# Linear attention with a gated one-token FFN: kv times wo in full matmuls, an earlier normalisation, and another order of the first loads

## The chip, the cores and the metric

The kernel runs on one core of one Trainium2 chip. The metric is the time on the device in microseconds (us), median of three runs. A profile of one execution stands beside it, with a trace of every instruction. TensorE is the matrix engine (PE in the profile, PEld its weight loads), VectorE is DVE, ScalarE is ACT, GpSimd is POOL, and SyncE (SP) issues most of the transfers. Each engine works through its own queue in order and waits for others by semaphores.

## The reference

The input x has 2048 tokens of 1024 numbers, in bf16. Path A is linear attention with 32 heads of 32 numbers; path B feeds the one token with the highest router score through a gated FFN and adds the result to that token alone; a sigmoid gate per token mixes the two. Cut to what matters:

```python
qkv = x @ wqkv                                  # 2048 x 3072, split in q, k, v of 32 heads x 32
phi = lambda t: where(t > 0, t + 1, exp(t)) + 1e-6
pq, pk = phi(q), phi(k)
kv  = einsum("bhsd,bhse->bhde", pk, v)          # 32 x 32 for each head
z   = einsum("bhsd->bhd", pk)
num = einsum("bhqd,bhde->bhqe", pq, kv)
den = einsum("bhqd,bhd->bhq", pq, z) + 1e-6
a   = (num / den) @ wo                          # heads side by side, then 1024 x 1024
# B: idx = argmax(x @ w_r); y = (silu(x[idx] @ w_gate) * (x[idx] @ w_up)) @ w_down
#    b = x with sigmoid(r[idx]) * y added to row idx
g   = sigmoid((x * gate_w).sum(-1))
out = g * a + (1 - g) * b
```

The kernel never forms num: it divides pq by den, multiplies kv by wo once (M, 1024 x 1024), and the output is pq times M.

## The kernel before

P is 128, D 1024, NG and KC are 8 (groups of 128 columns, four heads each), NT is 16 (tiles of 128 tokens). The start: loads, the transposes of the first two x tiles on TensorE, and the first K products, which run along with the K rows of the weights as they land.

```python
    load_x(0, 1)
    load_k(0)
    load_x(1, 1)
    for c in range(1, KC):
        load_k(c)
    for t in (2, 3):
        sp.dma_start_transpose(out=xT[:, :, t * P : (t + 1) * P], in_=x2d[t * P : (t + 1) * P, :])
    for c in (0, 4):
        sp.dma_start(out=wkv[:, c : c + 4, D : 2 * D], in_=wqkv_v[:, c : c + 4, 2 * D : 3 * D])
...
    warm_sb = const.tile([P, 512], BF)
    dve.memset(warm_sb[:], 0.0)
...
    def phi_exp(ps):
        u = tmp.tile([P, 512], F32, tag="phi_u")
        act.activation(u[:], ps, ACTF.Relu, scale=-1.0, bias=LN1EPS)
        e = tmp.tile([P, 512], F32, tag="phi_e")
        act.activation(e[:], u[:], ACTF.Exp, scale=-1.0, bias=LN1EPS)
        return e

    def phi_dve(ps, e0, out_ap):
        dve.scalar_tensor_tensor(out_ap, ps, EPS, e0[:], op0=ALU.max, op1=ALU.add)
...
    def unit_Q(g, j, pinned=False):      # phi of 128 columns of q for 512 tokens, transposed
        ps = ps_work.tile([P, 512], F32, tag="w")          # ps_work: four PSUM banks
...
    def warm(n):
        for _ in range(n):
            pe.matmul(warm_ps[:], lhsT=warm_sb[:, 0:P], rhs=warm_sb[:], start=True, stop=True)

    warm(N_WARM)
...
    def first_mm(t, c0, c1):
        for c in range(c0, c1):
            for nb in range(2):
                kv_mm(first[t][nb], t, nb, c, c + 1)
...
    unit_T(0)
    first_mm(0, 0, 1)
    unit_T(1)
    warm(1)
    for c in range(1, KC):
        first_mm(0, c, c + 1)
        if c < KC - 1:
            first_mm(1, c - 1, c)
    es = [phi_exp(first[0][nb][:]) for nb in range(2)]
...
    for t in (2, 3):
        kv_open(t)
        for nb in range(2):
            ps = ps_t.tile([P, 512], F32, tag="t")
            kv_mm(ps, t, nb, 0, KC)
            kv_evac(ps, t, nb)
```

After that come V of the first four tiles, the router, K, V and kv sums of the other twelve with Q units and the FFN among them (not touched by the change). Then the part between the last kv sum and the output:

```python
    for i in range(3):
        n = 3 if i < 2 else 2
        acc3 = kvacc[i][:, 0 : 129 * n].rearrange("p (g e) -> p g e", e=129)
        dve.tensor_copy(kvbd[:, 3 * i : 3 * i + n, :], acc3[:, :, 0:128])
...
    wo = pb.tile([P, 2, 4, D], BF)
    wo_v = A_wo.rearrange("(hf r c e) n -> hf r e c n", hf=2, r=4, c=4)
    for hf in range(2):
        for r in range(4):
            nc.sync.dma_start(out=wo[32 * r : 32 * r + 32, hf, :, :], in_=wo_v[hf, r])
    kvT = pb.tile([P, 2, 4, 32], BF)
...
    def den_group(pair):                 # denominators of 1024 tokens, 16 matmuls, then
...                                      # dn on ScalarE, and on VectorE
        dve.reciprocal(rd[:], dn[:])
        for hh in range(4):
            eng = nc.sync if hh % 2 == 0 else nc.gpsimd
            eng.dma_start(out=rdp[pair][32 * hh : 32 * hh + 16, :], in_=rd[hh : P : 8, :])
        return rdp[pair]
...
    def norm_step(n):
        for _ in range(n):
            if not norm_units:
                return
            rd, g, j = norm_units.popleft()
            rb = tmpb.tile([P, 512], F32, tag="rb", bufs=4)
            dve.stream_shuffle(rb[:], rd[:], [8 * (j % 2) + g] * 32)
            sl = pq_all[:, g, 512 * j : 512 * j + 512]
            nc.gpsimd.tensor_tensor(sl, sl, rb[:], op=ALU.mult)

    def unit_M(hf, nh):
        pm = [ps_den.tile([P, 512], F32, tag="d", name=f"pm{r}") for r in range(3)]
        pm.append(ps_ffn.tile([P, 512], F32, tag="f", name="pm3"))
        strict[0] = True
        for c in range(4):
            for r in range(4):
                pe.matmul(pm[r][32 * c : 32 * c + 32, :], lhsT=kvT[32 * r : 32 * r + 32, hf, c, :],
                          rhs=wo[32 * r : 32 * r + 32, hf, c, 512 * nh : 512 * nh + 512],
                          start=True, stop=True, tile_position=(32 * r, 32 * c))
        strict[0] = False
        for r in range(4):
            eng = dve.tensor_copy if r % 2 else act.copy
            eng(m_sb[:, 4 * hf + r, 512 * nh : 512 * nh + 512], pm[r][:])

    rdA = den_group(0)
    unit_Q(*q_units.popleft())
    pt = ps_den.tile([P, NG, P], BF, tag="d")
    for g in range(NG):
        pe.transpose(pt[:, g, :], kvbd[:, g, :], ident[:])
    for c in range(4):
        for r in range(4):
            eng = dve.tensor_copy if r % 2 else act.copy
            eng(kvT[32 * r : 32 * r + 32, :, c, :], pt[32 * c : 32 * c + 32, r:NG:4, 32 * c : 32 * c + 32])
    normalise(rdA, 0)
    normalise(rdA, 1)
    g_m = 0
    nq_done = 0
    while q_units:
        unit_Q(*q_units.popleft(), pinned=True)
        nq_done += 1
        if g_m < 4 and nq_done > 5 and nq_done % 2 == 0:
            unit_M(g_m // 2, g_m % 2)
            g_m += 1
        if nq_done % 3:
            norm_step(1)
...
    for t in range(NT):                  # output: 16 matmuls of 512 columns for each tile
...
            for g in range(NG):
                pe.matmul(ps[:, 0:cw], lhsT=pq_all[:, g, t * P : (t + 1) * P], rhs=m_sb[:, g, c0 : c0 + cw], ...)
            dve.scalar_tensor_tensor(ot[:, c0 : c0 + cw], ps[:, 0:cw], gate[:, t : t + 1], xg[:, c0 : c0 + cw], ...)
...
        if t == 0:
            rdB = den_group(1)
            normalise(rdB, 2)
            normalise(rdB, 3)
        norm_step(NORM_PER_T[t])
```

A normalisation step is a shuffle on VectorE, which spreads a row of reciprocals over the partitions of its head, and a multiplication on GpSimd in place; the output matmul of a tile needs it for all eight groups. ps_work has four banks, ps_ffn one; ps_t (three banks) serves the start and ps_den (three) the end. Where `strict[0]` is set, TensorE keeps program order; elsewhere a scheduler places the instructions when the program is built.

## Time and profile before

| what | value |
|---|---|
| time, median of 3 | 263.29 us (262.69 to 263.72) |
| span of the profiled run | 261.1 us |
| TensorE | 250.6 us busy, 96% |
| VectorE | 151.4 us, 58% |
| ScalarE | 125.4 us, 48% |
| GpSimd | 46.4 us, 18% |
| matmul for K and V, 128x512 | 465 in the records |
| matmul for the output, 128x512 | 259 in the records |
| multiplication on GpSimd, 128x512 | 32, 1163 ns each |
| shuffle on VectorE, 128x512 | 32, 733 ns each |
| reciprocal on VectorE, 128x512 | 2, 3.35 us each |

A few per cent of the matmul records are missing from the trace. The end of a matmul is modelled: one of 512 columns is shown with 379 ns, but the next one starts 0.2157 us after it at full clock, so counts are multiplied by the distance of the starts. In lines of a group the columns are: line, engine, operation, output and input, shapes and count, then busy time with the mean of one, then the idle time of the engine ahead of it and what ended it. In a timeline the first column is the start and the second the length, both in us. Nearly all instructions go through one recording helper and so carry its line, L75; they are told apart by the names of their tiles.

### The profile page before, as it was taken

The page shows a single profiled execution, that of the slowest core. Times are in us where ns is not written, and L with a number is a line of the kernel's source. Part 1 is how long each engine was busy: PE and PEld are TensorE (multiplying, and loading weights), DVE is VectorE, ACT ScalarE, POOL GpSimd, SP SyncE. Part 2 cuts the span into 40 slices and gives each one's busy share as a digit, 9 for nine tenths or more (in the row PEclk, how much of TensorE's full clock was granted, in tenths as well). Part 3 has the DMA queues.
Part 4 walks back from the last instruction along what each step waited for, and adds up shares of the span by engine and source line. Part 5 has one row for each costly group of instructions (what it writes and reads, how often), then busy time and mean ns, then how long its engine had stood idle before and what let it go on. Part 6 is the DMA issues. An engine that isn't in the chain of part 4 may idle for free.

```text
span 261.1 us, 3892 instructions
## 1 busy us (share of the span) xinstructions
PE 250.6 (96%) x1444; PEld 115.8 (44%) x1471; DVE 151.4 (58%) x254; ACT 125.4 (48%) x202; POOL 46.4 (18%) x94
## 2 busy tenths in 40 slices
PE   7999999999999999999999999999995999999994
PEld 4444454444444444444444444444441344444443
DVE  1055033323173326699999942587599699974443
ACT  2195324646445354445553735579883442242310
POOL 5000001010000000000000000110059469990000
PEclk9999999999999999999999999999999799999999
DMA  6999980029999989997970000990001174545222
GB/s 221 268 343 233 227 321 1 0 13 350 348 348 343 326 263 335 348 392 250 465 251 0 3 0 0 248 209 9 3 1 40 45 252 128 161 151 173 80 80 80
DMA packets 47369, 47.71 MB, mean 183 GB/s; under 512 B 18476, under 2 KB 35252, under 8 KB 47288
## 3 DMA queue, kind: packets, MB, share of 16 engines
q1 hardware_dynamic: 47064, 47.34, 60.0%
q8 instruction: 11, 0.18, 0.3%
q0 software_dynamic: 256, 0.14, 0.2%
q14 instruction: 6, 0.05, 0.1%
q10 hardware_dynamic: 32, 0.00, 0.0%
HBM read 39.34 MB, written 8.40 MB: 183 GB/s over the span
## 4 chain that ended last, share of the span: by engine, by line
PE 74%; DVE 14%; issue 3%; POOL 3%; DMA 3%; ACT 2%; DVEq 0%; POOLq 0%; SPq 0%
PE ps L75 65%; DVE yacc L75 10%; POOL pq_all L556 3%; DMA wt<-in_B_w_down_dram 3%; PE first L75 3%; PE kvacc L75 2%; ACT u L75 1%; DVE pk L75 1%; PE warm_ps L75 1%; DVE rb L75 1%; ACT e L75 1%; PE dps L75 1%; DVE pq_all L75 1%; PE rps L75 1%; PE pst L75 0%
## 5 line engine op out<-in xcount | busy, mean ns | idle before, releaser
L75 PE MATMUL ps<-wkv,xT 128*128 128x512 bf16 x465 | 107.1, 379 | 1.2 <-DVE pk L75 0.4
L75 PEld LDWEIGHTS <-xT 128*128 128x128 bf16 x512 | 48.8, 98 | 59.9 <-issue 5.0
L75 PE MATMUL ps<-m_sb,pq_all 128*128 128x512 bf16 (+1 forms) x259 | 57.3, 379 | 3.4 <-POOL pq_all L556 2.2
L75 PE MATMUL ps<-xT,wq 128*128 128x512 bf16 x250 | 57.5, 379 | 0.9 <-issue 0.5
L75 ACT ACTIVATE u<-ps 128x512 f32<-128x512 f32 x60 | 35.8, 596 | 38.5 <-PE ps L75 37.2
L75 ACT ACTIVATE e<-u 128x512 f32<-128x512 f32 x64 | 40.3, 630 | 2.3 <-DVE pq_all L75 0.4
L75 PEld LDWEIGHTS <-pq_all 128*128 128x128 bf16 x264 | 25.9, 99 | 34.5 <-POOL pq_all L556 4.7
L556 POOL TENSOR_TENSOR pq_all<-pq_all,rb 128x512 bf16<-128x512 bf16 x32 | 36.1, 1163 | 20.3 <-PE ps L75 17.8
L75 PEld LDWEIGHTS <-wq 128*128 128x128 bf16 x256 | 24.5, 98 | 30.3 <-issue 2.0
L75 ACT CAST vt<-ps 128x512 bf16<-128x512 f32 x32 | 18.8, 587 | 36.0 <-PE ps L75 34.8
L75 DVE SCALAR_TENSOR_TENSOR yacc<-wt,hcol,yacc 128x1024 f32<-128x1024 bf16 x27 | 34.5, 1279 | 0.5
L75 DVE SCALAR_TENSOR_TENSOR pq_all<-ps,e 128x512 bf16<-128x512 f32 x32 | 21.9, 685 | 18.9 <-ACT e L75 18.6
L75 DVE SCALAR_TENSOR_TENSOR ot<-ps,gate,xg 128x512 bf16<-128x512 f32 (+1 forms) x33 | 23.7, 725 | 15.7 <-PE ps L75 15.7
L75 DVE SCALAR_TENSOR_TENSOR pk<-ps,e 128x512 bf16<-128x512 f32 x28 | 19.1, 685 | 21.9 <-ACT e L75 21.9
L75 ACT ACTIVATE xg<-xt,omg 128x1024 f32<-128x1024 bf16 x16 | 18.1, 1146 | 25.8 <-DVE ot L75 25.8
L75 DVE STREAM_SHUFFLE rb<-rdp 128x512 f32<-128x512 f32 x32 | 22.2, 733 | 0.0
L205 POOL MEMSET vt<- 128x8 bf16 x16 | 1.9, 137 | 108.4 <-PE kvacc L75 108.4
L75 PEld LDWEIGHTS <-pk 128*128 128x128 bf16 x128 | 8.5, 98 | 3.3 <-issue 0.4
L75 PE MATMUL kvacc<-vt,pk 128*128 128x129 bf16 x128 | 9.7, 221 | 0.0
L75 PE MATMUL first<-wkv,xT 128*128 128x512 bf16 x31 | 7.8, 400 | 0.1
L75 DVE SCALAR_TENSOR_TENSOR pk<-first,e 128x512 bf16<-128x512 f32 x4 | 2.8, 692 | 8.6 <-ACT e L75 8.6
L75 DVE CAST r_bf<-rps 128x512 bf16<-128x512 f32 x1 | 0.7, 690 | 12.0 <-PE rps L75 12.0
(97 smaller groups left out, 87.5 us busy)
## 6 DMA issues: line engine op xcount, KB each, us to landing
wt<-in_B_w_down_dram SPq DMA_DIRECT2D x14, 512.0 KB, 6.4
wt<-in_B_w_gate_dram SPq DMA_DIRECT2D x8, 512.0 KB, 8.1
wt<-in_B_w_up_dram SPq DMA_DIRECT2D x8, 512.0 KB, 8.7
xt<-xp SPq DMA_DIRECT2D x16, 256.0 KB, 3.1
out_dram<-ot SPq DMA_DIRECT2D x15, 256.0 KB, 2.0
wt<-in_B_w_gate_dram SPq DMA_DIRECT2D x8, 384.0 KB, 6.8
wt<-in_B_w_up_dram SPq DMA_DIRECT2D x8, 384.0 KB, 5.4
wkv<-in_A_wqkv_dram SPq DMA_DIRECT2D x8, 256.0 KB, 4.7
```

Source lines behind the costliest of these rows:

```text
L75: inst = fn(*a, **k)
L205: nc.gpsimd.memset(vt_t[t][:, :, 128:129], 1.0)
L556: nc.gpsimd.tensor_tensor(sl, sl, rb[:], op=ALU.mult)
```

## The change

It has four parts. First, kv times wo: before, the 32x32 blocks of kv are cut out of the transposed matrix by 16 small copies and multiplied with permuted rows of wo by sixteen tiles of the array at once; now kv is multiplied by a block-diagonal mask on the way out of PSUM, transposed whole, and each group of 128 rows is multiplied with its own 128 rows of wo by two full matmuls, whose results all leave through ScalarE. wo comes in its natural order by one transfer. Second, the normalisation: one step after every Q unit, not after two of three, and another table of steps for the output tiles; Q units are no longer pinned to program order. Third, the start: the clock of TensorE is warmed on constants that exist when the program starts, instead of on a tile that VectorE has to clear; two K rows of the weights are loaded and used ahead of the second x tile, and narrow warming matmuls stand before them. Fourth, the K sums of the fourth token tile go to the work banks instead of the three banks of the transposes. The aim is fewer waits of TensorE at the start and ahead of the output.

```diff
--- before.py
+++ after.py
@@ -28,11 +28,11 @@
 NG = D // P
 EPS = 1e-6
 LN1EPS = math.log1p(EPS)
-N_WARM = 5
+N_WARM = 6
 Q_PER_T = {4: 2, 5: 1, 6: 1, 7: 2, 8: 1, 9: 1, 10: 2, 11: 1, 12: 1, 13: 2, 14: 1, 15: 0}
 FFN_PER_T = {6: (0, 4), 7: (4, 4), 8: (4, 4), 9: (4, 4), 10: (4, 2), 11: (2, 2), 12: (1, 2), 13: (1, 2), 14: (1, 2), 15: (1, 0)}
 FFN_DEPTH = 9
-NORM_PER_T = [2, 2, 2, 2, 2, 2, 2, 2, 2, 2, 2, 1, 0, 0, 0, 0]
+NORM_PER_T = [2, 0, 0, 3, 3, 3, 3, 3, 3, 3, 3, 3, 3, 3, 3, 3]
 
 
 @with_exitstack
@@ -125,8 +125,9 @@
 
     load_x(0, 1)
     load_k(0)
+    load_k(1)
     load_x(1, 1)
-    for c in range(1, KC):
+    for c in range(2, KC):
         load_k(c)
     for t in (2, 3):
         sp.dma_start_transpose(out=xT[:, :, t * P : (t + 1) * P], in_=x2d[t * P : (t + 1) * P, :])
@@ -136,13 +137,14 @@
         sp.dma_start_transpose(out=xT[:, :, 512 * g4 : 512 * g4 + 512], in_=x2d[512 * g4 : 512 * g4 + 512, :])
     sp.dma_start(out=wq[:], in_=wqkv_v[:, :, 0:D])
 
-    warm_sb = const.tile([P, 512], BF)
-    dve.memset(warm_sb[:], 0.0)
-
     ident = const.tile([P, P], BF)
     make_identity(nc, ident[:])
     nc.scalar.dma_start(out=wrg_rows[0:8, :], in_=B_w_r.rearrange("(c p) -> c p", p=P))
     nc.scalar.dma_start(out=wrg_rows[8:16, :], in_=gate_w.rearrange("(c p) -> c p", p=P))
+    mask_bd = const.tile([P, P], F32)
+    nc.gpsimd.memset(mask_bd[:], 0.0)
+    for i in range(4):
+        nc.gpsimd.memset(mask_bd[32 * i : 32 * i + 32, 32 * i : 32 * i + 32], 1.0)
     nc.gpsimd.memset(mzc[:], 0.0)
     for hh in range(4):
         for g0 in range(4):
@@ -227,20 +229,21 @@
                              start=False, stop=False, skip_group_check=True)
         del pk_t[t], vt_t[t]
 
-    def unit_Q(g, j, pinned=False):
+    def unit_Q(g, j):
         ps = ps_work.tile([P, 512], F32, tag="w")
-        strict[0] = pinned
         for c in range(KC):
             pe.matmul(ps[:], lhsT=wq[:, c, g * P : (g + 1) * P], rhs=xT[:, c, 512 * j : 512 * j + 512],
                              start=(c == 0), stop=(c == KC - 1))
-        strict[0] = False
         phi_evac(ps[:], pq_all[:, g, 512 * j : 512 * j + 512])
 
     warm_ps = ps_ffn.tile([P, 512], F32, tag="f")
 
-    def warm(n):
+    warm_w = nc.const_aps.tensor(1.0, (P, P), BF)
+    warm_x = nc.const_aps.tensor(1.0, (P, 512), BF)
+
+    def warm(n, w=512):
         for _ in range(n):
-            pe.matmul(warm_ps[:], lhsT=warm_sb[:, 0:P], rhs=warm_sb[:], start=True, stop=True)
+            pe.matmul(warm_ps[:, 0:w], lhsT=warm_w, rhs=warm_x[:, 0:w], start=True, stop=True)
 
     warm(N_WARM)
     kv_open(0)
@@ -253,13 +256,14 @@
                 kv_mm(first[t][nb], t, nb, c, c + 1)
 
     unit_T(0)
-    first_mm(0, 0, 1)
+    warm(3, 128)
+    first_mm(0, 0, 2)
     unit_T(1)
-    warm(1)
-    for c in range(1, KC):
+    for c in range(2, KC):
         first_mm(0, c, c + 1)
         if c < KC - 1:
-            first_mm(1, c - 1, c)
+            first_mm(1, c - 2, c - 1)
+    first_mm(1, 5, 6)
     es = [phi_exp(first[0][nb][:]) for nb in range(2)]
     first_mm(1, 6, 8)
     for nb in range(2):
@@ -269,7 +273,8 @@
     for t in (2, 3):
         kv_open(t)
         for nb in range(2):
-            ps = ps_t.tile([P, 512], F32, tag="t")
+            pool, tag = (ps_t, "t") if t == 2 else (ps_work, "w")
+            ps = pool.tile([P, 512], F32, tag=tag)
             kv_mm(ps, t, nb, 0, KC)
             kv_evac(ps, t, nb)
     ps_t_cm.__exit__(None, None, None)
@@ -503,17 +508,15 @@
     for i in range(3):
         n = 3 if i < 2 else 2
         acc3 = kvacc[i][:, 0 : 129 * n].rearrange("p (g e) -> p g e", e=129)
-        dve.tensor_copy(kvbd[:, 3 * i : 3 * i + n, :], acc3[:, :, 0:128])
+        dve.tensor_tensor(kvbd[:, 3 * i : 3 * i + n, :], acc3[:, :, 0:128],
+                                mask_bd[:].unsqueeze(1).to_broadcast([P, n, P]), op=ALU.mult)
     ph1.close()
 
     pb = ctx.enter_context(tc.tile_pool(name="pb", bufs=1))
     m_sb = pb.tile([P, NG, D], BF)
-    wo = pb.tile([P, 2, 4, D], BF)
-    wo_v = A_wo.rearrange("(hf r c e) n -> hf r e c n", hf=2, r=4, c=4)
-    for hf in range(2):
-        for r in range(4):
-            nc.sync.dma_start(out=wo[32 * r : 32 * r + 32, hf, :, :], in_=wo_v[hf, r])
-    kvT = pb.tile([P, 2, 4, 32], BF)
+    wo = pb.tile([P, NG, D], BF)
+    nc.sync.dma_start(out=wo[:], in_=A_wo.rearrange("(g p) n -> p g n", p=P))
+    kvT = pb.tile([P, NG, P], BF)
     rdp = [pb.tile([P, 512], F32, name=f"rdp{i}") for i in range(2)]
     for r in rdp:
         nc.gpsimd.memset(r[:], 1.0)
@@ -555,41 +558,32 @@
             sl = pq_all[:, g, 512 * j : 512 * j + 512]
             nc.gpsimd.tensor_tensor(sl, sl, rb[:], op=ALU.mult)
 
-    def unit_M(hf, nh):
-        pm = [ps_den.tile([P, 512], F32, tag="d", name=f"pm{r}") for r in range(3)]
-        pm.append(ps_ffn.tile([P, 512], F32, tag="f", name="pm3"))
-        strict[0] = True
-        for c in range(4):
-            for r in range(4):
-                pe.matmul(pm[r][32 * c : 32 * c + 32, :], lhsT=kvT[32 * r : 32 * r + 32, hf, c, :],
-                          rhs=wo[32 * r : 32 * r + 32, hf, c, 512 * nh : 512 * nh + 512],
-                          start=True, stop=True, tile_position=(32 * r, 32 * c))
-        strict[0] = False
-        for r in range(4):
-            eng = dve.tensor_copy if r % 2 else act.copy
-            eng(m_sb[:, 4 * hf + r, 512 * nh : 512 * nh + 512], pm[r][:])
+    def unit_M(g):
+        for nh in range(2):
+            ps = ps_den.tile([P, 512], F32, tag="d")
+            pe.matmul(ps[:], lhsT=kvT[:, g, :], rhs=wo[:, g, 512 * nh : 512 * nh + 512], start=True, stop=True)
+            act.copy(m_sb[:, g, 512 * nh : 512 * nh + 512], ps[:])
 
     rdA = den_group(0)
     unit_Q(*q_units.popleft())
     pt = ps_den.tile([P, NG, P], BF, tag="d")
     for g in range(NG):
         pe.transpose(pt[:, g, :], kvbd[:, g, :], ident[:])
-    for c in range(4):
-        for r in range(4):
-            eng = dve.tensor_copy if r % 2 else act.copy
-            eng(kvT[32 * r : 32 * r + 32, :, c, :], pt[32 * c : 32 * c + 32, r:NG:4, 32 * c : 32 * c + 32])
+    dve.tensor_copy(kvT[:], pt[:])
     normalise(rdA, 0)
     normalise(rdA, 1)
     g_m = 0
     nq_done = 0
     while q_units:
-        unit_Q(*q_units.popleft(), pinned=True)
+        unit_Q(*q_units.popleft())
         nq_done += 1
-        if g_m < 4 and nq_done > 5 and nq_done % 2 == 0:
-            unit_M(g_m // 2, g_m % 2)
+        if g_m < NG and nq_done > 6:
+            unit_M(g_m)
             g_m += 1
-        if nq_done % 3:
-            norm_step(1)
+        norm_step(1)
+    while g_m < NG:
+        unit_M(g_m)
+        g_m += 1
     phq.close()
 
     fin = ctx.enter_context(tc.tile_pool(name="fin", bufs=3))
```

## The prediction

> **What bounds the kernel now.** I read the page first. TensorE is busy 96% of the span, and in the chain that ended last it holds 74%, with a VectorE piece of 14% in the middle (the down projection). So time can come from three places only: matmuls that vanish, matmuls at half clock, and the few places where TensorE stands idle. Three rows of the 40 slices show where the last two are:
>
> ```profile
> PE   7999999999999999999999999999995999999994
> POOL 5000001010000000000000000110059469990000
> PEclk9999999999999999999999999999999799999999
> ```
>
> Slice 0 (the start) and slices 30 and 31 (195.8 to 208.9 us) are the weak ones; there GpSimd has just started to work, and the clock drops with it. Next I read the timeline of TensorE in that stretch:
>
> ```profile
> 194.82 1.03 PE L75 MATMUL ps<-xT,wq 128*128 128x512 bf16 x4
> 196.81 1.31 PE L75 MATMUL ps<-m_sb,pq_all 128*128 128x512 bf16 x5 [0.97 <-DVE pq_all L75]
> 198.85 0.39 PE L75 MATMUL ps<-m_sb,pq_all 128*128 128x512 bf16 x1 [0.73 <-POOL pq_all L556]
> 199.97 0.39 PE L75 MATMUL ps<-m_sb,pq_all 128*128 128x512 bf16 x1 [0.73 <-POOL pq_all L556]
> 201.09 3.47 PE L75 MATMUL ps<-m_sb,pq_all 128*128 128x512 bf16 x9 [0.73 <-POOL pq_all L556]
> 204.49 1.32 PE L75 MATMUL dps<-pq_all,zc 128*32 128x512 bf16 x16
> 205.75 1.04 PE L75 MATMUL ps<-m_sb,pq_all 128*128 128x512 bf16 x3
> ```
>
> The first output tile is fed one 128-token group at a time: after each matmul it waits for GpSimd to normalise the next slice (about 1.12 us from one start to the next). The four idles add up to 3.16 us. Then 9 matmuls take 3.47 us where at 0.2157 us each they would take 1.94: single starts lie 0.427 us apart from 201.8 to 204.0, and the trace has the clock at half from 201.69 to 205.10. Why GpSimd is late is in its own row and in VectorE's:
>
> ```profile
> 192.01 12.38 POOL L556 TENSOR_TENSOR pq_all<-pq_all,rb 128x512 bf16<-128x512 bf16 x11 [17.84 <-PE ps L75]
> 189.93 1.28 DVE L75 CAST m_sb<-pm 128x512 bf16<-128x512 f32 x2
> 191.14 0.72 DVE L75 STREAM_SHUFFLE rb<-rdp 128x512 f32<-128x512 f32 x1
> ```
>
> The reciprocal was done at 172.6 and its four spreading loads had landed by 178.4, but in VectorE's queue the first shuffle stands behind six of the eight m_sb evictions, so it starts at 191.14. The start of the kernel:
>
> ```profile
> 1.43 2.31 PE L75 MATMUL warm_ps<-warm_sb 128*128 128x512 bf16 x5 [1.43 <-DVE warm_sb L75]
> 3.54 1.06 PE L75 MATMUL pst<-ident,xnat 128*128 128x128 bf16 x8
> 4.69 1.03 PE L75 MATMUL first<-wkv,xT 128*128 128x512 bf16 x2
> 5.52 1.06 PE L75 MATMUL pst<-ident,xnat 128*128 128x128 bf16 x8
> 6.37 0.63 PE L75 MATMUL warm_ps<-warm_sb 128*128 128x512 bf16 x1
> 19.18 1.89 PE L75 MATMUL ps<-wkv,xT 128*128 128x512 bf16 x8 [0.40 <-DVE pk L75]
> ```
>
> All matmuls before 7.1 us run at half clock (0.427 us for 512 columns). The 0.40 us at 19.18 is the second half of the fourth tile's K: its PSUM tile is the fourth taken from a pool of three, so it waits for the third tile's first half to be evicted.
>
> **What the Trainium skill says.** "TensorE: Matmul & The Clock Gate", section "What's actually happening": the clock is halved or full by how busy TensorE was in a window of 3.413 us that runs freely and does not start with the kernel. The trace agrees: half clock lasts 3.41 us, starts lie 0.427 or 0.2157 us apart. "TensorEngine Tiling (Array Packing)", section "PSUM Bottleneck": tiling speeds up TensorE and not the eviction of PSUM. It agrees: 16 concurrent 32x32 matmuls take 0.36 us, their four evictions 0.53 to 0.68 us each. "SBUF — State Buffer", section "Door 1: The DMA port swizzle": 32 partitions reach half the ports, measured there as 189 GB/s. The eight loads of wo (256 KB, 32 partitions each) land from 165.4 to 177.7 us, 170 GB/s. Same page, "Who interferes with whom": a VectorE instruction with one SBUF input and no two-port mode does not contend with GpSimd; from 212 to 231 us the multiplications stay at 1.13 us each beside shuffles and output evictions, which agrees.
>
> **The change, part by part.** The built order of both kernels shows the queues; durations are from the trace.
>
> *Kv times wo.* Removed: four groups of 16 tiled matmuls, 4 x 0.36 = 1.44 us, with three idles of 0.16 us around them. Added: 16 full matmuls, 16 x 0.2157 = 3.45 us, two after each Q unit from the seventh on. TensorE alone would lose 1.5 us. For this, 8 evictions leave VectorE (8 x 0.6 = 5 us) and all 16 go to ScalarE; the 16 small kvT copies (8 x 0.19 on VectorE, 8 x 0.20 on ScalarE, interleaved with the phi work) become one copy, about 0.75 us, estimated from the 0.42 us of a 512-wide bf16 eviction. The mask multiply replaces casts of the same size (0.55 us for 384 columns) and I give it nothing.
>
> *Normalisation.* The first two shuffles now stand right behind the third evicted Q unit, and all 16 of the first pair stand before the last five Q evictions. The wo load is now one transfer over 128 partitions and should be gone by about 172 us, so the spreads land at about 175.5. GpSimd needs 16 x 1.125 = 18 us, from about 176.5 to 194.6. In the new order the output stage begins later than that:
>
> - Q units from 169.63: 14 x 8 x 0.2157 = 24.16 us; with 3.45 us for kv times wo this ends at 197.2.
> - First output tile 16 x 0.2157 = 3.45 us, the second denominator at full clock 1.13 us (0.97 + 0.16, as at 167.4).
> - The second tile starts at 201.9 instead of 205.75: 3.9 us less.
>
> The half-clock stretch goes with the idles, since nothing starves the window. I keep 0.2 us back for small waits, so 3.7 us.
>
> *Fourth tile in work banks.* Its two PSUM tiles reuse slots whose evictions end at 14.5 and 15.7, and it starts at about 17: the wait of 0.40 us goes. The V units behind it wait for evictions of the second tile and of the fourth, which end at about 17, 18, 21.5 and 22.5; TensorE comes there at 20.5, 22.2, 24 and 25.7. No new wait.
>
> *Start.* Warm matmuls on constants begin at about 1.0 instead of 1.43, and six end at about 3.6; x lands at 3.42, so nothing is gained there. Three narrow warm matmuls (3 x 0.107) fill the 0.30 us before the first K product. Two K rows ahead of the second x tile: four products instead of two plus one wide warm one. With the clock rising at 7.13 as in this run, the second transposes end at 7.3 and 28 products of 0.2157 us remain, which would end at 13.35 against 13.44. But K row 3 lands at 8.46, and the new order asks for it after 8 products (about 8.2) where the old asks after 10 (8.69). From 8.5, 24 products remain: 13.7. I therefore give the start nothing: between 0.1 gained and 0.3 lost if the clock rises as here, and up to 0.5 gained where the free-running window had treated the old start worse.
>
> *Between.* From 21 to 165 us the instruction order is the same. The transposing loads of x end at 32.8 and are first needed in full at 35.0, so an earlier TensorE is not held up; the down projection's loads are released by TensorE's own matmuls at about 99.7, so that whole piece moves along. From the second output tile on, the work is the same 52 us plus the tail.
>
> Sum: 3.7 + 0.4 = 4.1 us, give or take the start. From the median 263.29 this is 259.2; from the profiled run, 262.69, it is 258.6. I take 258.9, or 1.7% less.
>
> **Rivals.** *ScalarE becomes the bound in the kv-times-wo stretch.* For it: all 16 evictions are there, between phi halves. Per Q unit ScalarE needs 0.47 to 0.53 for each eviction and about 0.5 and 0.63 for the two phi halves, 2.0 to 2.1 us in all, against 2.16 us of TensorE. It is close: with the full 0.587 of an isolated cast it would be 2.4, eight units would lose up to 1.9 us, and the time would be about 260.8. Against it: in the trace consecutive starts on ScalarE lie 0.47 to 0.54 apart.
>
> *VectorE, in order, stalls on GpSimd.* A shuffle needs one of four rb buffers, so the tenth waits for the sixth multiplication, the fifteenth for the eleventh, and Q evictions queue behind. I work out the ninth Q eviction up to 2.8 us late; four work banks (1.7 to 2.2 us each) cover this. If not, the idle only moves 10 us earlier: 260 to 261. After the second denominator, 16 shuffles stand among 8 output evictions (3 per tile asked for instead of 2), VectorE needs 1.93 us per eviction against 1.73 of TensorE; four banks absorb that, as they do now from 214 to 231.
>
> *The tiled product was worth more than the wait it caused.* If the normalisation still came late, +1.5 us of TensorE work would show: 264 to 265. The order of the queues speaks against it.
>
> *It gives more.* If the window costs the unprofiled runs before more at the start, 257.5.
>
> **Range and chances.** The one large term, 3.7 to 3.9 us, rests on counted matmuls and on two in-order queues with 2 to 3 us of slack; the small ones are worth 0.5 either way. 8 in 10: 257.6 to 260.5. The 2% line is at 258.0, just below my value: faster 0.20, same 0.77, slower 0.03.
>
> **What would show it.** Right: the first shuffle at about 176; 16 multiplications done before the last Q unit; no idle of TensorE over 0.3 us between 165 and 206; clock 1.00 there; 16 m_sb casts on ScalarE with kv times wo at 3.4 us; no wait at about 19; K row 3's wait at about 8.2. Wrong: idles before the new matmuls with ScalarE as releaser, Q units waiting for pq_all evictions near 185 to 192, or a first output tile that still waits for GpSimd.

## The result and the profile after

The changed kernel takes 259.88 us (median of 4 runs, 259.61 to 260.84) against 263.15 for the kernel before beside it (4 runs, 262.69 to 263.72): a ratio of 0.9881, 95% interval 0.9848 to 0.9914, so it is faster by 1.2% and short of the 2% line. The traced runs took 259.61 and 262.69 us, their spans are 258.0 and 261.1 us. Four stretches, taken on TensorE, make up the whole difference of 3.10 us between the traces:

| stretch on TensorE | before, us | after, us | difference |
|---|---|---|---|
| span's start to the first V matmul | 21.12 | 20.69 | -0.43 |
| from there to the first Q unit after the transposes of kv (169.63, 170.53) | 148.51 | 149.84 | +1.33 |
| from there to the second output tile (205.75, 202.68) | 36.12 | 32.15 | -3.97 |
| from there to the end of the span | 55.35 | 55.32 | -0.03 |

The prediction had the first row at -0.4, the second at 0 and the third at -3.7. Three rows of the 40 slices of the changed kernel, as they were shown of the kernel before:

```profile
PE   7999999999999999999999999999999999999994
POOL 6000001010000000000000000104994029960000
PEclk9999999999999999999999999999999999999999
```

The weak slices 30 and 31 are gone from TensorE's row, the clock is full to the end, and GpSimd now starts its block of work two slices earlier. The timeline of TensorE in the same stretch, after (start, length, instruction, count; in brackets idle time before it):

```profile
182.61 0.59 PE L75 MATMUL ps<-wo,kvT 128*128 128x512 bf16 x2
183.04 1.89 PE L75 MATMUL ps<-xT,wq 128*128 128x512 bf16 x8
...
197.72 0.59 PE L75 MATMUL ps<-wo,kvT 128*128 128x512 bf16 x2
198.15 3.62 PE L75 MATMUL ps<-m_sb,pq_all 128*128 128x512 bf16 x15
201.70 1.05 PE L75 MATMUL dps<-pq_all,zc 128*32 128x512 bf16 x16
202.68 7.51 PE L75 MATMUL ps<-m_sb,pq_all 128*128 128x512 bf16 x33
```

No line has a wait. Each pair of full matmuls for kv times wo takes 0.43 us from start to start, eight of them 3.45; the first output tile takes 3.55 instead of 7.68 and the denominator after it 0.98 instead of 1.26. The timelines of VectorE and GpSimd say why:

```profile
177.52 0.01 DVE L75 LOAD_MASK_SELECT rb<-rdp  x1 [1.36 <-DMA rdp<-rd]
177.54 0.73 DVE L75 STREAM_SHUFFLE rb<-rdp 128x512 f32<-128x512 f32 x1
178.17 0.02 DVE L75 LOAD_MASK_SELECT rb<-rdp  x1
...
178.42 18.03 POOL L559 TENSOR_TENSOR pq_all<-pq_all,rb 128x512 bf16<-128x512 bf16 x16 [3.35 <-DVE rb L75]
```

The first shuffle is now held by the spread of the reciprocals and by nothing else (191.14 before, 177.54 after), and the sixteen multiplications end at 196.45, 1.7 us ahead of the first output tile. The start, on TensorE's timeline:

```profile
1.02 2.72 PE L75 MATMUL warm_ps<-const-bfloat16-1.0 128*128 128x512 bf16 x6 [1.02 <-PEq L629]
3.67 1.04 PE L75 MATMUL pst<-ident,xnat 128*128 128x128 bf16 x8
...
6.18 0.87 PE L75 MATMUL first<-wkv,xT 128*128 128x512 bf16 x2 [0.29 <-DMA wkv<-in_A_wqkv_dram]
...
13.58 7.07 PE L75 MATMUL ps<-wkv,xT 128*128 128x512 bf16 x32
```

The first K products end at 13.58 instead of 13.44, and the block behind them runs through where it had a wait of 0.40 us. A wait that the prediction did not have stands at 6.18, for the second K row; the one that it did have (K row 3, at about 8.2) is not there.

Then the row that was predicted as zero. These are the places in TensorE's timeline of the changed kernel, between 60 and 145 us, that carry a wait for another engine or a transfer:

```profile
73.44 0.40 PE L75 MATMUL ps<-wt,xs_pad 128*32 128x512 bf16 x4 [0.19 <-DMA wt<-in_B_w_gate_dram]
...
119.90 3.75 PE L75 MATMUL ps<-wkv,xT 128*128 128x512 bf16 x15 [0.25 <-DVE pq_all L75]
142.42 2.89 PE L75 MATMUL ps<-xT,wq 128*128 128x512 bf16 x12 [0.31 <-DVE pk L75]
```

They are small, and with others too short to be printed they add up: the changed kernel is 0.43 us ahead at 72.4, 0.06 ahead at 73.8, 0.36 behind at 119.9 and 0.90 behind from 142.4 on. The waits at 119.9 to 142.4 are for VectorE, which from 107 to 151 us works on the down projection (28 steps of 1.28 us, with evictions between them). The Q unit at 142.42 is called "the Q unit behind the down projection" below, though 5 of the 28 steps start after it. The first step, before and then after:

```profile
106.47 0.75 DVE L75 TENSOR_SCALAR yacc<-wt,hcol 128x1024 f32<-128x1024 bf16 x1 [4.33 <-DMA wt<-in_B_w_down_dram]
```

```profile
107.37 0.75 DVE L75 TENSOR_SCALAR yacc<-wt,hcol 128x1024 f32<-128x1024 bf16 x1 [5.28 <-DMA wt<-in_B_w_down_dram]
```

The first W_down load landed at 107.24 instead of 106.35, though its issue was done at 100.51 instead of 100.97: it stood behind other weights. Going back along the stream of FFN weights, the loads land 0.5 to 1.1 us late as far back as those at 66 us, and the stream itself begins with a row that GpSimd fetches once the router has chosen it. GpSimd's timeline, before and after:

```profile
40.37 0.72 POOL L329 DMA_DIRECT2D c<-cand  x1 [1.15 <-DVE cand L75]
52.21 0.49 POOL L350 DMA_DIRECT2D xsel_row<-in_A_x_dram  x1 [11.12 <-DVE pq_all L75]
```

```profile
39.94 0.72 POOL L334 DMA_DIRECT2D c<-cand  x1 [1.15 <-DVE cand L75]
53.85 0.49 POOL L355 DMA_DIRECT2D xsel_row<-in_A_x_dram  x1 [13.19 <-issue]
```

The candidates leave GpSimd 0.43 us earlier than before, and the row fetch 1.64 us later. "issue" means that the profile shows nothing that GpSimd waited for. Instruction by instruction, the register move ahead of the fetch is at 51.57 before and at 51.52 after; the fetch follows 0.63 us later before and 2.33 us later after. In that gap of the changed kernel an 8 KB packet on one of the two instruction queues arrives, at 52.13; in the kernel before one arrives at 53.63, when the fetch is out. The only thing that the change did to GpSimd ahead of this point is five more fills (the mask tile). So the theory for the experiments (A): **five more instructions moved the place where GpSimd must wait for its next stretch of program to just ahead of the fetch on which the weight stream hangs.**

### The profile page after: what moved, and what is told of

It is laid out like the page before. It is cut to its first block, busy times and chain, and to the rows that moved or that the text cites. A ratio compares the mean times of both kernels' runs of the same rounds, so it can differ in the third digit from the quotient of the medians.

```text
span 258.0 us, 3788 instructions
## 1 busy us (share of the span) xinstructions
PE 251.0 (97%) x1399; PEld 116.9 (45%) x1426; DVE 145.1 (56%) x238; ACT 127.1 (49%) x202; POOL 47.0 (18%) x99
## 4 chain that ended last, share of the span: by engine, by line
PE 69%; DVE 13%; DMA 9%; issue 4%; SPq 3%; ACT 0%; POOLq 0%; POOL 0%; DVEq 0%
PE ps L75 62%; DVE yacc L75 10%; DMA wt<-in_B_w_gate_dram 4%; DMA wt<-in_B_w_down_dram 3%; PE first L75 3%; SPq L383 2%; PE kvacc L75 2%; DMA wkv<-in_A_wqkv_dram 2%; DVE pq_all L75 1%; DVE pk L75 1%; PE dps L75 1%; PE rps L75 1%; DMA xsel<-in_A_x_dram 1%; SPq L75 0%; POOLq L354 0%
## 5 line engine op out<-in xcount | busy, mean ns | idle before, releaser
L75 PE MATMUL ps<-xT,wq 128*128 128x512 bf16 x251 | 58.4, 379 | 0.6 <-DVE pk L75 0.3
L75 PE MATMUL ps<-m_sb,pq_all 128*128 128x512 bf16 (+1 forms) x258 | 55.3, 372 | 0.3
L75 ACT CAST m_sb<-ps 128x512 bf16<-128x512 f32 x16 | 9.3, 583 | 0.0
L75 PE MATMUL ps<-wt,xs_pad 128*32 128x512 bf16 (+1 forms) x128 | 7.7, 355 | 0.2 <-DMA wt<-in_B_w_gate_dram 0.2
```

The costliest lines, as they stand in the source:

```text
L75: inst = fn(*a, **k)
```

## The experiments

Comparisons with the kernel before are ratios of runs on one chip. Its runs spread widely (79 of them lie from 260.5 to 264.4; four slow ones, up to 265.6, are left out), so the traces carry most of the readings below.

### The mask's fills on VectorE, and the same fills in the kernel before

```diff
     mask_bd = const.tile([P, P], F32)
-    nc.gpsimd.memset(mask_bd[:], 0.0)
+    dve.memset(mask_bd[:], 0.0)
     for i in range(4):
-        nc.gpsimd.memset(mask_bd[32 * i : 32 * i + 32, 32 * i : 32 * i + 32], 1.0)
+        dve.memset(mask_bd[32 * i : 32 * i + 32, 32 * i : 32 * i + 32], 1.0)
```

> The changed kernel, with the five fills of the mask tile on VectorE instead of GpSimd; nothing else. Theory A (the gain of the start is lost because five more GpSimd instructions move the point at which GpSimd fetches its next stretch of instructions to just ahead of the router's row fetch): the row fetch is issued at about 51.8 us instead of 53.85, the first down-projection step on VectorE starts at about 106.0 instead of 107.37, the Q unit behind the down projection at about 141.1 instead of 142.42, and the time is 258.5 (258.2 to 258.9). Rival B (the weight stream or the memory is simply slower in the changed kernel, whatever GpSimd does): row fetch earlier but first down-projection step still at about 107.3, time unchanged at 259.9.

Measured: 258.76 us (6 runs, 258.5 to 259.7), ratio 0.9859 (0.9809 to 0.9908). Row fetch at 51.87, first down-projection step at 106.57, Q unit behind it at 141.63; the last two half a microsecond later than expected. GpSimd's timeline:

```profile
51.87 0.49 POOL L355 DMA_DIRECT2D xsel_row<-in_A_x_dram  x1 [11.13 <-DVE pq_all L75]
52.84 0.57 POOL L356 DMA_DIRECT2D xsel<-in_A_x_dram  x1 [0.49 <-issue]
```

The opposite edit puts the five GpSimd fills, of a tile that nothing reads, into the kernel before:

```diff
+    mask_bd = const.tile([P, P], F32)
+    nc.gpsimd.memset(mask_bd[:], 0.0)
+    for i in range(4):
+        nc.gpsimd.memset(mask_bd[32 * i : 32 * i + 32, 32 * i : 32 * i + 32], 1.0)
     nc.gpsimd.memset(mzc[:], 0.0)
```

> The kernel before, plus the five GpSimd fills of a mask tile that nothing reads; nothing else. Theory A: the instruction fetch falls ahead of the row fetch here too, the row fetch is issued about 1.6 us later than in the kernel before (53.8 instead of 52.2), the first down-projection step starts at 107.4 to 107.9 instead of 106.47, and the time is 264.1 to 264.6. Rival B: the fills end long before they matter, nothing moves, 263.15.

Measured: 263.25 us (14 runs, 261.65 to 266.07), ratio 1.0027 (0.9993 to 1.0061). The time expected, 264.1 to 264.6, was missed, and the interval holds both no loss and one of 0.9 us: in the time alone no answer. In the trace there is one:

```profile
54.60 0.49 POOL L354 DMA_DIRECT2D xsel_row<-in_A_x_dram  x1 [13.22 <-issue]
55.22 0.57 POOL L355 DMA_DIRECT2D xsel<-in_A_x_dram  x1
```

The fetch is 2.39 us later than in the kernel before: 1.7 us of it is the longer gap behind the register move, the rest a move that came later itself (0.30 of that is a later start of this run); the first down-projection step comes at 109.22 instead of 106.47. Five fills that end some 50 us earlier moved the fetch in both directions, so rival B's "nothing moves" is out; that the fills cost time in the kernel before is not shown.

### The weight stream without the router's row ahead of it

```diff
             if t == 4 and i == 0:
                 router_part1()
-                gate_logits()
                 ffn_prefetch()
+                gate_logits()
```

(The queue order of the weight loads now hangs on the load of wq.) The fills stay on GpSimd.

> The changed kernel, with the first nine FFN weight loads queued on SyncE ahead of the load of the gate logits that waits for the router's row. Theory A (the weight stream is released by the row fetch and from then on is bound by the transfer rate): the first gate weight is issued well before 55 us, the first down-projection step starts at 105 or earlier, and the time is 258.0 to 258.7 although the row fetch is still late. Rival C (the weights' buffers, freed by TensorE, set the pace, not the start of the stream): first down-projection step unchanged at 107.3, time 259.9.

Measured: 259.07 us (6 runs, 258.48 to 259.78), ratio 0.9869 (0.9819 to 0.9920). The row fetch is as late as in the changed kernel (53.99), the first nine weights are issued between 31 and 47 us, and the first down-projection step starts at 106.47, not at 105 or earlier. So half of the expectation missed: once the stream no longer hangs on the row, the loads wait for buffers that TensorE's matmuls free, and W_down lands when it did in the kernel before. But the late row fetch cost nothing here, which is what theory A needs: from the end of K's first block to the Q unit behind the down projection this run takes 120.93 us against 121.84.

### The start and the work banks alone

The kernel before with only the edits for the warm matmuls, the K rows, the order of the first products and the work banks; the mask, kv times wo and the normalisation as before:

```diff
     load_k(0)
+    load_k(1)
     load_x(1, 1)
...
-    first_mm(0, 0, 1)
+    warm(3, 128)
+    first_mm(0, 0, 2)
     unit_T(1)
-    warm(1)
...
-            ps = ps_t.tile([P, 512], F32, tag="t")
+            pool, tag = (ps_t, "t") if t == 2 else (ps_work, "w")
+            ps = pool.tile([P, 512], F32, tag=tag)
```

> The kernel before with only the change's start (warm matmuls on constants, two K rows ahead of the second x tile) and the fourth tile's K sums in work banks; the mask, kv times wo, the load of wo and the normalisation as before. Theory A: GpSimd's program is as before, so the 0.43 us won by 21 us is carried through router, weight stream and down projection: 262.6 to 262.9. Rival B (the stream swallows any gain of the start): down projection not earlier than before, 263.15.

Measured: 261.90 us (22 runs, 260.6 to 263.8), ratio 0.9988 (0.9962 to 1.0014). In the trace TensorE is 0.86 us ahead at 20.1 us and 0.26 ahead at 141.3; the row fetch follows its move by 0.63 us. So part of a gain at the start is lost on the way to the down projection even with the fetch in place. In the time it is not to be seen: the median lies under the 262.6 to 262.9 expected, but the interval holds 1.

### The changed kernel again

> The changed kernel once more, unedited, for runs beside the others on this chip. Theory A (five more GpSimd fills move its instruction fetch ahead of the row fetch): the row fetch is again issued near 53.9 us, the first down-projection step again near 107.3, 259.5 to 260.2. Rival B (the late row fetch was an accident of the one traced run): row fetch at about 51.8, first down-projection step at about 106.4, 258.8.

Measured: 259.94 us (14 runs, 258.82 to 261.1), ratio 0.9887 (0.9859 to 0.9916). Row fetch at 53.80, first down-projection step at 107.61: no accident of one trace.

On a third chip the changed kernel and the one with the fills on VectorE ran side by side:

> The changed kernel with the mask fills on VectorE, once more, beside the changed kernel on the same chip. Theory A: row fetch again at about 51.8, 0.7 to 1.5 us faster than the changed kernel's run of the same chip (258.5 to 259.2 against about 259.9). Rival B: no difference in the medians.

> The changed kernel, unedited, as the partner of the two other runs on this chip. Theory A: row fetch near 53.8, 259.6 to 260.2. Rival B: as the run with the fills on VectorE.

Measured: 259.14 us (6 runs, 258.51 to 260.78) and 259.83 us (5 runs, 259.49 to 260.5). The medians differ by 0.69 us, just under what A expected. Row fetch 0.63 and 2.56 us behind its move. (At 53.57 the fetch of the first is late on the clock because that traced run, the slowest of its six, began late: its first K products ended at 15.36.) All runs together, 258.88 (12) with the fills on VectorE and 259.90 (19) with them on GpSimd: about 1.0 us, over three chips, of which only the last had both.

One table of all traces, by where the fills are. "Gap" is from the register move to the row fetch, "stretch" from the transpose of the router's weights (20 to 22 us) to the Q unit behind the down projection (140 to 144 us), all in us:

| fills on GpSimd | gap | stretch | none on GpSimd | gap | stretch |
|---|---|---|---|---|---|
| changed kernel | 2.33 | 121.84 | kernel before | 0.63 | 120.52 |
| changed, second trace | 2.35 | 122.18 | start only | 0.63 | 121.12 |
| changed, third trace | 2.56 | 122.40 | fills on VectorE | 0.64 | 120.98 |
| before with fills | 2.35 | 122.98 | fills on VectorE, again | 0.63 | 121.24 |
| wo in eight | 2.33 | 121.50 | tiled, early | 0.63 | 120.94 |
| wo in eight, pinned | 2.32 | 120.45 | tiled, spread copies | 0.63 | 121.11 |
| weights first | 2.45 | 120.93 | tiled, balanced | 0.64 | 121.20 |

The gap has two values and nothing between them, and in all seven traces on the left an 8 KB instruction packet arrives inside it, in all seven on the right after the fetch is out. The seven long gaps end 1.71 to 1.82 us after that packet, the longest (2.56) too, where the packet came latest. The stretch has a median of 121.8 on the left and 121.1 on the right; leaving out the run whose stream does not hang on the fetch, 122.0 on the left. One run on the left, "wo in eight, pinned", does not fit: its fetch is late and its stretch short. Its last eight loads up to the first of W_down took 10.0 us to land, where those of the other runs took 10.6 to 12.4; why was not found. So the late fetch costs about 0.9 us as a rule, not in every run.

### wo in eight loads

```diff
-    nc.sync.dma_start(out=wo[:], in_=A_wo.rearrange("(g p) n -> p g n", p=P))
+    wo_v = A_wo.rearrange("(hf g p) n -> hf p g n", hf=2, p=P)
+    for hf in range(2):
+        for r in range(4):
+            nc.sync.dma_start(out=wo[32 * r : 32 * r + 32, 4 * hf : 4 * hf + 4, :], in_=wo_v[hf, 32 * r : 32 * r + 32])
```

> The changed kernel, with wo loaded in eight pieces of 32 partitions each, same rows to same partitions; nothing else. Built so, the scheduler puts the first eleven shuffles behind eleven of the fourteen Q evictions again instead of behind two. Theory D (the gain at the transition is the place of the shuffles in VectorE's queue, and the single load of wo is what gives it): the first shuffle starts at about 195, the first output tile waits for GpSimd as in the kernel before, the stretch from the first Q unit after the transposes to the second output tile takes 36 to 38 us instead of 32.15, and the time is 264 to 266. Rival E (full matmuls with evictions on ScalarE are what gained it): that stretch stays at 32 to 33 us, the time within 0.7 us of the changed kernel.

Measured: 265.63 us (4 runs, 264.99 to 266.23), ratio 1.0111 (1.0034 to 1.0187). Slower than both kernels, from one load cut in eight. On VectorE's timeline the first shuffle, and on TensorE's the first output tile:

```profile
192.46 0.69 DVE L75 SCALAR_TENSOR_TENSOR pq_all<-ps,e 128x512 bf16<-128x512 f32 x1 [1.12 <-ACT e L75]
...
193.08 0.73 DVE L75 STREAM_SHUFFLE rb<-rdp 128x512 f32<-128x512 f32 x1
```

```profile
197.88 1.07 PE L75 MATMUL ps<-m_sb,pq_all 128*128 128x512 bf16 x4
199.69 0.39 PE L75 MATMUL ps<-m_sb,pq_all 128*128 128x512 bf16 x1 [0.73 <-POOL pq_all L562]
...
208.03 2.33 PE L75 MATMUL ps<-m_sb,pq_all 128*128 128x512 bf16 x10
```

The waits of 0.73 us for GpSimd are back, four of them, and the stretch to the second output tile takes 37.8 us (170.25 to 208.03). The shuffles were not late because wo was late, for the spread of the reciprocals had landed at 179.56: the built program puts them behind eleven Q evictions as soon as wo comes in eight pieces. To tell the transfer from the order, the next run keeps the eight pieces and pins the shuffles to the places that they have in the changed kernel (`strict[0]` holds the Q units and kv times wo of this loop in program order with them):

```diff
     while q_units:
+        strict[0] = True
         unit_Q(*q_units.popleft())
         nq_done += 1
+        norm_step({3: 2, 4: 1, 5: 2, 6: 2, 7: 3, 8: 2, 9: 3, 10: 1}.get(nq_done, 0))
         if g_m < NG and nq_done > 6:
             unit_M(g_m)
             g_m += 1
-        norm_step(1)
+        strict[0] = False
```

> The changed kernel, with wo in eight pieces as in the run before, but the shuffles pinned to the places in VectorE's queue that they have in the changed kernel (behind the third Q eviction after the transposes, the last Q evictions behind all sixteen). Theory D: the spread of the reciprocals lands at about 178.5 to 179.5 instead of 177.4, the multiplications end at 197 to 198, still in time for the first output tile: the stretch takes 32.1 to 32.8 us and the time is within 0.7 us of the changed kernel. Rival F (the transfer of wo by itself, not the order, is worth the time): 262 or more.

Measured: 259.61 us (17 runs, 257.56 to 261.56), ratio 0.9894 (0.9869 to 0.9918), a stretch of 32.19 us (168.39 to 200.58). The order of the queue is worth all of it and the shape of the transfer by itself nothing.

### Tiled kv times wo, with the shuffles early

Sixteen 32x32 tiles over permuted wo rows, eight loads and small kvT copies, all as in the kernel before, but the shuffles pinned early and all sixteen evictions on ScalarE:

```diff
     while q_units:
+        strict[0] = True
...
-        if g_m < NG and nq_done > 6:
-            unit_M(g_m)
+        norm_step({4: 1, 5: 2, 6: 2, 7: 1, 8: 2, 9: 2, 10: 2, 11: 2, 12: 2}.get(nq_done, 0))
+        if g_m < 4 and nq_done > 6 and nq_done % 2 == 1:
+            unit_M(g_m // 2, g_m % 2)      # sixteen 32x32 tiles, evicted by act.copy
```

> The changed kernel, with kv times wo put back as sixteen concurrent 32x32 tiles over permuted wo rows (eight loads, small kvT copies, no mask multiply, so no mask fills on GpSimd), but with all its evictions on ScalarE and the shuffles pinned early in VectorE's queue, one or two behind each Q eviction from the fourth on. Theory D: the first output tile starts 2.0 us earlier than in the changed kernel (3.45 us of TensorE become 1.44), nothing waits for GpSimd, the stretch takes 30.2 to 30.8 us instead of 32.15, and with the row fetch back at about 51.9 the time is 256.5 to 257.3: tiling was never the trouble, the queue was. Rival E (tiling itself brings the waits): 259 or more, with waits before the tiled matmuls or before the first output tile.

Measured: 258.98 us (4 runs, 258.81 to 260.38), ratio 0.9868 (0.9791 to 0.9945); a stretch of 32.47 us. The expectation missed by 1.7 us, and TensorE's timeline names them:

```profile
178.11 5.34 PE L75 MATMUL ps<-xT,wq 128*128 128x512 bf16 x23 [1.67 <-DVE pq_all L75]
```

The sixteen small kvT copies stand in one block here, alternating between VectorE and ScalarE and each waiting for the other engine (0.45 us a pair), and Q evictions queue behind them. In the next run they are spread, four behind each of the first four Q units:

```diff
+        if nq_done <= 4:
+            kvt_copies(nq_done - 1)
```

> As the tiled run before (sixteen concurrent 32x32 tiles, shuffles early, evictions on ScalarE, no mask fills), but with the sixteen small kvT copies spread, four behind each of the first four Q units, instead of in one block, in which VectorE and ScalarE waited for each other 3.6 us and TensorE then 1.67 us. Theory D: that wait goes, the stretch from the first Q unit after the transposes to the second output tile takes 30.6 to 31.0 us (32.15 in the changed kernel, less 1.44 of TensorE's work), and the time is 257.0 to 257.8. Rival E: another wait of the tiled form takes its place, and the stretch stays at 32 or more.

Measured: 259.53 us (5 runs, 259.4 to 259.89), ratio 0.9871 (0.9828 to 0.9915); a stretch of 32.60 us. That wait went and another came. TensorE's and ScalarE's timelines:

```profile
186.14 1.74 PE L75 MATMUL pm<-wo,kvT 32*32 32x512 bf16 x16
187.82 3.63 PE L75 MATMUL ps<-xT,wq 128*128 128x512 bf16 x16
191.38 0.76 PE L75 MATMUL pm<-wo,kvT 32*32 32x512 bf16 x16
```

```profile
185.38 2.03 ACT L75 CAST m_sb<-pm 128x512 bf16<-128x512 f32 x4
187.28 0.63 ACT L75 ACTIVATE u<-ps 128x512 f32<-128x512 f32 x1
187.94 0.63 ACT L75 ACTIVATE e<-u 128x512 f32<-128x512 f32 x1
...
189.62 2.03 ACT L75 CAST m_sb<-pm 128x512 bf16<-128x512 f32 x4
```

A group of sixteen tiles takes 1.74 us instead of 0.43: its last tiles come when ScalarE has emptied the banks of the group before (casts until 187.4). ScalarE has no idle time: four casts to the next four casts is 4.24 us, for two Q units that with the tiled group take TensorE 3.92. So ScalarE sets the pace of this stretch (theory G). The Trainium skill has the case ("TensorEngine Tiling (Array Packing)", section "PSUM Bottleneck"): after the speedup the PSUM copy may be the limit, and both ScalarE and VectorE should do it. The 4.24 us against 3.92 agree with the first half. The last run does that, and moves the kvT copies and some shuffles as well:

```diff
-            eng = dve.tensor_copy if r % 2 else act.copy      # kvT copies
-            eng(kvT[32 * r : 32 * r + 32, :, c, :], ...)
+            dve.tensor_copy(kvT[32 * r : 32 * r + 32, :, c, :], ...)
...
-            eng = act.copy                                    # m_sb evictions
+            eng = dve.tensor_copy if r == 3 else act.copy
-        norm_step({4: 1, 5: 2, 6: 2, 7: 1, 8: 2, 9: 2, 10: 2, 11: 2, 12: 2}.get(nq_done, 0))
+        norm_step({4: 1, 5: 1, 6: 2, 7: 1, 8: 1, 9: 1, 10: 2, 11: 1, 12: 2, 13: 1}.get(nq_done, 0))
```

> As the tiled run with spread kvT copies, but the small kvT copies all on VectorE, one in four of the m_sb evictions on VectorE and three on ScalarE, and the shuffles more evenly spread (one or two per Q unit). Theory G (in this stretch ScalarE and VectorE set the pace: two phi halves and two m_sb casts take ScalarE 2.1 us per Q unit, so the 1.44 us of TensorE that tiling saves are not to be had unless evictions move): with ScalarE at 3.8 us and VectorE at 3.7 us per two Q units against 3.81 us of TensorE, the stretch takes 30.8 to 31.3 us instead of 32.5, no wait before the tiled matmuls over 0.3 us, and the time is 257.5 to 258.3. Rival E (tiling itself brings the waits): the stretch stays at 32.2 to 32.8 and the time at 259.0 to 259.6.

Measured: 257.16 us (5 runs, 256.79 to 257.63), ratio 0.9794 (0.9740 to 0.9848), faster than the kernel before, by some 2%, and than the changed one (none of whose runs, on other chips, was under 258.82). TensorE's timeline:

```profile
181.82 0.43 PE L75 MATMUL pm<-wo,kvT 32*32 32x512 bf16 x16
182.18 3.63 PE L75 MATMUL ps<-xT,wq 128*128 128x512 bf16 x16
185.74 0.43 PE L75 MATMUL pm<-wo,kvT 32*32 32x512 bf16 x16
...
195.69 3.62 PE L75 MATMUL ps<-m_sb,pq_all 128*128 128x512 bf16 x16
199.24 1.05 PE L75 MATMUL dps<-pq_all,zc 128*32 128x512 bf16 x16
```

The groups take 0.43 us and lie 3.92 us apart, and the stretch takes 30.58 us (169.64 to 200.22), 1.57 less than in the changed kernel; in the stretch of the table above it is another 0.6 ahead (121.20 against 121.84). Tiling was not the trouble. Three things were moved at once, so which of them removed the wait was not separated.

## Why the prediction was right or wrong

The value, 258.9, lies 1.0 us under the measured 259.88, and the range holds it. Between the two traces 4.1 us were expected and 3.1 came.

**The transition: right, 3.97 us against 3.7 to 3.9, and for the reason given.** The place of the shuffles in VectorE's queue decides it: with the transfer changed and the place kept, 32.19 us; with the place lost, 37.8. Two things about it were not as written. The step "the wo load is now one transfer over 128 partitions and should be gone by about 172 us" failed: it landed from 165.85 to 176.65, 10.8 us for 2 MB (194 GB/s), where the eight had taken 12.8 (164.95 to 177.72), and the spread landed at 177.33 instead of 175.5. In the six traces with one load it took 9.0 to 10.8 us, never the 6 to 7 that the step needs. It did no harm, because the multiplications had 1.7 us to spare. And 1.6 of the 3.97 us is the stretch at half clock, which does not come in every run of the kernel before: the traces of the start-only kernel and of the kernel before with fills have the same four idles (3.16 us) and full clock, and take 34.48 and 34.50 us. The last three lines of that stretch in the start-only kernel, whose counterparts at 201.09 and 204.49 in the kernel before took 3.47 and 1.32 us:

```profile
199.71 0.39 PE L75 MATMUL ps<-m_sb,pq_all 128*128 128x512 bf16 x1 [0.72 <-POOL pq_all L559]
200.83 2.12 PE L75 MATMUL ps<-m_sb,pq_all 128*128 128x512 bf16 x9 [0.73 <-POOL pq_all L559]
202.88 1.05 PE L75 MATMUL dps<-pq_all,zc 128*32 128x512 bf16 x16
```

Of 79 runs of the kernel before beside the experiments, 29 had a mean granted clock of 0.991 to 0.995 (median 263.37 us) and 50 one of 0.997 or more (261.90). Against the latter the change is worth some 2 us. That the traced run of the kernel before was one of the slower kind is luck that helped the number: without the half clock the stretch would have given some 2.3 us and not 3.97. The changed kernel ran at 0.998 or more in each of its 23 runs.

**Kv times wo in full matmuls: the cost was right, the sum behind it by luck.** The 3.45 us were measured to the digit and ScalarE did not stall. But "TensorE alone would lose 1.5 us" is 3.45 less 1.44 less three idles of 0.16 us, and these idles are misread. They stand ahead of blocks from which a record is missing, as here, where the program has 16 matmuls:

```profile
184.60 3.40 PE L75 MATMUL ps<-xT,wq 128*128 128x512 bf16 x15 [0.16 <-issue]
```

The trace of the start-only kernel, the same in this stretch, has all 112 matmuls of the Q units and no such idle. (The denominator's "0.97 + 0.16" is the same slip: it took 0.98.) What is there is another 0.11 us for each tiled group: from group to group it is 3.92 us, where 0.36 and 16 x 0.2157 make 3.81. So four groups cost 1.88 us, and the full matmuls cost 1.57 more, which is what the balanced tiled run got back. That they could be had back was not seen; it took a quarter of the casts, the kvT copies and the shuffles moved together.

**ScalarE as the bound** did not come true in the changed kernel (2.16 us of TensorE a unit hide its 2.0 to 2.1), and came true one edit away, at 2.12 us a unit against 1.96.

**The fourth tile in work banks: right.** The wait of 0.40 us is gone.

**The start, given nothing: right as a sum, wrong in its detail.** +0.14 us at the end of the first K products. In the twelve traces with the new start these end at 12.84 to 15.36, median 13.59, against 13.44 and 13.74 in the two with the old one. The wait came at K row 1 (0.29 us) and not at K row 3.

**The step that failed is "Between": "From 21 to 165 us the instruction order is the same", and "that whole piece moves along".** The order of TensorE is the same; GpSimd's got five fills longer, which the prediction did not count; they run from 1.1 to 2.2 us. They cost nothing when they run; as far as the packets tell, they cost by where the program behind them is cut into fetches. The row fetch came 2.3 instead of 0.63 us after its move, the weight stream began 1.2 us later (first gate weight issued at 56.70 instead of 55.45), and since that stream runs at some 350 GB/s (348 to 355 from 60 to 80 us in both traces) with little slack up to W_down, 0.9 us of it reached VectorE's down projection and through it TensorE. That the down projection's loads "are released by TensorE's own matmuls" is true of the issue, and the landing was decided by what stood ahead in the queue.

What stays open: the whole loss is 1.33 us, of which the fills explain about 0.9. The other 0.4 us is a gain of the start that does not reach the down projection in any trace with the new start and the fetch in place (stretch 120.9 to 121.2, against 120.52 in the one trace of the kernel before). Whether that trace was a quick one or whether buffers freed by TensorE and the transfer rate take the gain away was not settled. That the gap is a wait for the instruction packet is read from its time of arrival in fourteen traces; nothing here measures the fetch itself.

## What to carry to other kernels

When an order in a queue is left to a scheduler, look at the built order after every edit of a transfer or an eviction near it: with the same multiplications a stretch took 32.2 or 37.8 us by where sixteen shuffles stood. Count instructions added to an engine that later sits on a latency path, even where they run for free, and look for a changed idle with "issue" as its releaser ahead of the instruction on which transfers hang. And before matmuls are tiled or untiled, add up what the evicting engines need per unit of TensorE's work: 3.92 us of TensorE could be had only when neither ScalarE nor VectorE needed more.

## What the runs showed of the hardware that was not expected

- GpSimd stood 2.3 to 2.6 us between two instructions in seven traces and 0.63 to 0.64 in seven others; five fills some 50 us earlier decide which. In the long gaps an 8 KB instruction packet arrives 0.6 to 0.9 us after the move and 1.7 us or more ahead of the next instruction.
- The 2 MB of wo took 9.0 to 10.8 us as one load over 128 partitions (six traces, median 10.1) and 12.5 to 13.4 us as eight loads of 32 partitions (eight traces, median 13.1): about a quarter less, where the prediction had counted on about half.
- The same four idles of TensorE (0.97 and three of 0.73 us) bring 3.41 us at half clock with them in the trace of the kernel before and none in two others. Half clock for 3.41 of 261 us makes a mean of 0.993; 29 of 79 runs of the kernel before had such a mean, 50 did not, with 1.5 us between the medians. Where it fell in the runs without a trace is not known.
